# Two key tiles per P-times-V burst, and turns of four key tiles, in an attention and gated-FFN kernel

## The chip, the cores and the metric

The kernel runs on one core of one Trainium2 chip. The metric is the device time of one execution in microseconds (us). The engines are TensorE (PE, with its weight loads as PEld), VectorE (DVE), ScalarE (ACT), GpSimd (POOL), and SyncE (SP), whose queue issues the DMAs.

## The reference

One transformer block with adaptive layer norm, 2048 rows of 512, 32 heads of 16, one shared key and value head, and a gated FFN of width 1792 without a nonlinearity:

```python
mod = (silu(c) @ w_mod)                       # sa, ca, ga, sb, cb, gb
h = layernorm(x) * (1 + ca) + sa
q = (h @ wq) in 32 heads of 16;  k = h @ wk;  v = h @ wv      # k, v shared by the heads
p = softmax(q @ k.T / 4);  o = p @ v
x = x + ga * (o @ wo)
h = layernorm(x) * (1 + cb) + sb
x = x + gb * (((h @ w_gate) * (h @ w_up)) @ w_down)
```

## The kernel before, in words

**Units.** The attention is cut into NU = 32 units. A superblock is 256 queries (NS = 8 of them), and each has NC = 4 units of 8 heads. A unit passes over KT = 16 key tiles of 128 keys. For one key tile it needs four score products (two values of `p`, and two row groups `a` of the PE array: `a` = 0 is array rows 0 to 63, `a` = 1 rows 64 to 127), each 512 columns wide. ACT takes the exponential of each into one of eight SBUF buffers called `P` (`qk_exp`, L648 to L663). Then follow four products of V with those P tiles, which use all 128 rows and 32 columns each, so that the four run side by side (`pv`, L665 to L671). They are float32, and the profile counts two matmuls for each: a burst for one key tile is eight matmuls.

**Max.** Softmax needs the row maximum before the exponential. It comes from a second set of score products with queries as the output rows (`max_mm`, L593 to L611), whose 128 x 512 results DVE reduces (L605). They run about one unit ahead, and `flat` is the list of these steps. There are four of them for each key tile, as many as score products.

**Side products.** All other matrix products (the Q projection, the output projection `wo`, the FFN's gate and up `gu`, and its down product `down`) are cut into `Group`s (L491 to L538). A group accumulates into one PSUM bank, `n` steps on the upper and `n` on the lower row group of the array: 12 each for a `gu`, `wo` or Q group, 42 for a `down` group. One step on one row group is a "half". While row group 0 does score and max products, row group 1 does halves of a side group, and the two run at the same time. When a group goes on in the other row group than before, its first half there waits for an exponential of the turn before (`tc.add_manual_dep`, L527), so that the two row groups never write one bank at once. When a group has ended, `finish` gives it to its eviction: for a `gu` group ACT's copy L847, DVE's product L849, and POOL's L850 and L851.

**The order of the work.** It is written out by hand. `attend` (L1218) emits two key tiles in two turns. A string gives the order in a turn: `m` is a max product, `e` a score product with its exponential, `x` a side half; the digit is the row group, flipped in the second turn.

```python
MANY = "x1 e0 x1 m0 x1 e0 x1 e0 x1 m0 x1 m0 x1 m0 x1 e0"
```

So a turn in this style is eight slots, each with a half on one row group and an `m` or `e` on the other, and then `end_turn` emits the burst of one key tile. With `FEW` and `NO_SIDE`, used while the Q projections run or when no side group may begin, both row groups do `m` and `e`. `hooks` hangs the smaller work on fixed steps: weight preparation, and at `NORM_AT` the four parts of normalising the finished unit, whose P-times-V result `pv_out` has evicted. When `flat` is used up (in the last unit), `m` places take halves of a second group.

**PSUM.** All eight banks (NBANK) are in one queue, `pool` (L77 to L97). `ps_hold` takes the bank at the head and keeps it until `ps_give` appends it at the tail; `ps_mx` takes the head and appends it at once, so that score and max tiles rotate: a tile takes the bank of the tile as many places earlier as there are banks in the queue, and its matmul waits until the exponential or the reduce of that earlier tile is done. Held are one bank for the P-times-V result and one for each open side group, until its eviction has been emitted. `side_half` (L1203) keeps at most one group open in `cur`.

**Where the end comes from.** After the last unit a tail does the rest of the side products, with whole steps over all 128 rows.

Of the kernel before, what the change touches and what calls it, by code (L numbers as in the profile page):

```python
# [43 lines left out]
Q_LAG = 8  # L44
TR_WAIT = 11
NHF = 12
# [10 lines left out]

NO_SIDE = ("m0 m0 e1 m0 e1 e0 m1 e0 v", "e0 m1 m0 m1 e1 m1 e0 v e1")
FEW = "e1 m0 e0 x1 m0 x1 e0 x1 m0 x1 e1 m0"
MANY = "x1 e0 x1 m0 x1 e0 x1 e0 x1 m0 x1 m0 x1 m0 x1 e0"  # L60


@with_exitstack
def adaln_mqa_glu_kernel(ctx: ExitStack, tc: tile.TileContext, x_in, wq_in, wk_in, wv_in, wo_in,
# [35 lines left out]
        return ps_mx("misc", shape)  # L100


    c4 = consts.tile([KC, 128], F32, name="c4")
    nc.sync.dma_start(c4, c_in.rearrange("o (k p) -> (o k) p", p=128))
    wmA = big.tile([128, KC, 1536], F32, name="wmA", tag="wg")
# [7 lines left out]
    xbig = big.tile([128, 6, 2, D], F32, name="xbig", tag="wu")  # L113
    xts = [[xbig[:, i, t] for t in range(2)] for i in range(6)]
    for i in range(6, 8):
        xts.append([work.tile([128, D], F32, name="P", tag="P", bufs=8) for _ in range(2)])
# [12 lines left out]
    hf3 = [work.tile([128, BT], F32, name="P", tag="P", bufs=8) for k in range(KC)]  # L129
# [93 lines left out]
    h16 = big.tile([128, 2, KC, S], F16, name="h16", tag="big")  # L223
    kwb = big.tile([128, 2 * FT * D], F16, name="kwb", tag="wd")
    hfs = kwb[:, 0:2 * NHF * BT].bitcast(F32).rearrange("p (n t) -> p n t", n=NHF)
    ssqs = [kwb[:, 2 * n * BT:2 * n * BT + 2 * F].bitcast(F32) for n in (KC, 2 * KC)]
    kng = kwb[:, 2 * NHF * BT:2 * NHF * BT + BT]

# [412 lines left out]

    pvb = {}
    ptl = {}
    oc = {}
    och = {}
    pd = {}

    def qk_exp(u, kt, p, a, last=False):  # L648
        s = sst[u % 3]
        ptl[u, kt, p, a] = work.tile([128, D], F32, name="P", tag="P", bufs=8)  # L650
        t = ps_sc()
        keys = kst[64 * a:64 * a + 50, kt * 128:(kt + 1) * 128]
        if pending and last:
            for c in range(2):
                if c:
                    flush()
                nc.tensor.matmul(t[:, c * ST:(c + 1) * ST], keys, s[64 * a:64 * a + 50, c, p, :], start=True, stop=True)  # L657
        else:
            nc.tensor.matmul(t.rearrange("k (c n) -> k c n", c=2), keys, s[64 * a:64 * a + 50, :, p, :],  # L659
                             start=True, stop=True)  # L660
        ex = nc.scalar.activation(ptl[u, kt, p, a], t, AF.Exp)  # L661
        if sync["due"]:
            sync.update(due=False, exp=ex.ins.name)  # L663

    def pv(u, kt):  # L665
        if kt == 0:
            pvb[u] = ps_hold("pv")
        for j in range(4):
            p, a = divmod(j, 2)
            nc.tensor.matmul(pvb[u][32 * j:32 * j + 32, :], vst[:, kt, :], ptl[u, kt, p, a],  # L670
                             start=(kt == 0), stop=(kt == KT - 1))  # L671

    def pv_out(u):
        sb, ch = divmod(u, NC)
# [53 lines left out]
    def load_x(t):  # L728
        if t < KT - 2:
            x1s[t] = work.tile([128, D], F32, name="x1", tag="x1", bufs=6)  # L730
        else:
            x1s[t] = work.tile([128, D], F32, name="x1p", tag="P", bufs=8)
        nc.sync.dma_start(x1s[t], x_rows[t * 128:(t + 1) * 128, :])

    def wo_work(sb):
# [56 lines left out]
    def ln2_work(sb):  # L792
        st = {}

        def tr(i):
            def f():
                if not h2s:
                    h2T = big.tile([128, 2, 2, KC, ST], F16, name="h2T", tag="wq")
                    glus.append(big.tile([128, 2, 2, FT, ST], F16, name="glu", tag="big"))
                    h2s.update({s: h2T[:, s % 2] for s in range(NS)})  # L800
                st["p"] = ps_hold("mx")
                for k in range(2):
                    for t in range(2):
                        c = k * ST + t * 128
                        nc.tensor.transpose(st["p"][:, c:c + 128],  # L805
                                            n2s[2 * sb + t][:, (2 * i + k) * 128:(2 * i + k + 1) * 128], ident)
            return f

        def ev(i):
            def f():  # L810
                hf = work.tile([128, 2, ST], F32, name="hf", tag="g", bufs=2)
                for k in range(2):
                    nc.scalar.activation(hf[:, k, :], st["p"][:, k * ST:(k + 1) * ST], AF.Identity,  # L813
                                         bias=hsc[:, 2 * i + k, 0:1], scale=hsc[:, 2 * i + k, 1:2])
# [78 lines left out]
    def late_weights():  # L893
# [37 lines left out]
        def stage(n):  # L931
            if "d" in W:
                t = work.tile([128, D], F32, name="wsl", tag="xl", bufs=3)
            else:
                t = hfs[:, SLOTS[taken[0] % len(SLOTS)], :]
                taken[0] += 1
            nc.sync.dma_start(t[:, :sl[n][3]], sl[n][2])
            st[n] = t
# [262 lines left out]
    nrm = []  # L1201

    def side_half(r, cur=cur):  # L1203
        while True:
            if not cur:
                if cur is not second and second and second[0].turn != now[0]:
                    cur.append(second.pop())
                elif open_gate(now[0]):
                    cur.append(fill.popleft()[1])
                else:  # L1210
                    return
            if not cur[0].ended():
                break
            cur.clear()
        if cur[0].did[r] < cur[0].n:
            cur[0].half(r)

    def attend(u, kt):  # L1218


        now[0] = u * NSTEP + 2 * kt
        if cur and cur[0].ended():
            cur.clear()
# [5 lines left out]
        def end_turn(kt):  # L1229
            for g in ended:  # L1230
                g.finish()
            ended.clear()
            for f in ends:
                f()
            ends.clear()
            v = u * KT + kt - 1
            if v >= 0:
                pv(*divmod(v, KT))
                if v % KT == KT - 1:
                    ends.append(lambda: pv_out(u - 1))  # L1240
# [4 lines left out]
            hooks(u, 2 * kt + 1)  # L1245

        for turn in range(2):
            now[0] = u * NSTEP + 2 * (kt + turn)
            sync["before"] = sync["exp"]
            drain_posts()  # L1250
            order = orders[turn]
            for j, (what, a) in enumerate(order):
                if j == len(order) // 2:
                    drain_posts()
                    if style is not NO_SIDE:
                        late_max()
                    hooks(u, 2 * (kt + turn))
                a = a if style is NO_SIDE else a ^ turn
                if what == "m" and mstep[a] >= len(flat) and style is MANY:
                    mstep[a] += 1  # L1260
                    side_half(a, second)
                elif what == "m":
                    max_half(a)
                    drain_relus()
                elif what == "v":
                    end_turn(kt + turn)
                elif what == "x":
                    side_half(a)
                    continue
                else:  # L1270
                    k = count[a] = count.get(a, -1) + 1
                    qk_exp(u, kt + (k // 2 if style is MANY else turn), k % 2, a, j == len(order) - 1)
                flush()
            assert not sync["due"]
            if style is not NO_SIDE:
                end_turn(kt + turn)

    def hooks(u, i):
        step = u * NSTEP + i
# [1 line left out]
            b1, k = later_h.popleft()  # L1281
            h_halves(b1, (k,))
        side_step(step)
        if u > 0 and i in NORM_AT:
            if i == NORM_AT[0]:
                nrm[:] = normalise(u - 1)
            nrm[NORM_AT.index(i)]()
        if i == 20 and u > 0 and u % NC == 0:
            sb = u // NC - 1
            left = list(fill)  # L1290
            fill.clear()
# [7 lines left out]
    for u in range(NU):  # L1299
        if u == 1:  # L1300
            side.extend(dlist)
        for kt in range(0, KT, 2):
            attend(u, kt)

    def drain_all():
        for t in sorted(timers):
# [4 lines left out]

    u = NU - 1

    pv(u, KT - 1)
    pv_out(u)
    sync["before"] = sync["exp"]
    begun = cur + second
# [59 lines left out]
```

## Time and profile before

| | |
|---|---|
| median of 3 runs | 1665.57 us (1664.92 to 1665.84) |
| profiled execution: span from first to last instruction | 1663.8 us (the page gives no other time for it) |
| PE busy | 1643.3 us, 99% |
| DVE busy | 1402.3 us, 84% |
| ACT busy | 1234.8 us, 74% |
| POOL busy | 523.5 us, 31% |

A group of instructions is shown as line, engine, operation, output<-inputs, shapes, count, then busy time and mean length of one, then the idle time of its engine just before and what ended it. In rows in order of time the first number is the start in us from the start of the span, the second the length; `x4` means that four of a kind were merged into one row, which then reaches from the first one's start to the last one's end. PE matmuls overlap (their ends are modelled), so the distance between starts tells more than the length. The superblocks' regular stage lies between 320 and 1497 us; max products end at 1497 us and the units at 1552 us.

### The profile page before, as it was taken

What the parts mean: (1) busy time and instruction counts of PE and PEld (TensorE: products, weight loads), DVE (VectorE), ACT (ScalarE), POOL (GpSimd) and SP (SyncE); (2) the same over time, 40 slices, a digit from 0 to 9 for tenths busy, and PEclk for the clock granted to TensorE, in tenths of its full rate; (3) what the DMA queues carried; (4) which work ended last, traced back from release to release, by engine and by line L of the source; (5) the groups of instructions that cost most, each with busy time, mean ns of one, the idle gap of its engine ahead of it and who ended that gap; (6) DMA issues with size and microseconds to landing.
All of it is one profiled execution on the core that took longest, in us unless ns stands there. A gap on an engine that the chain in (4) does not pass through costs nothing.

```text
span 1663.8 us, 39821 instructions
## 1 busy us (share of the span) xinstructions
PE 1643.3 (99%) x15677; PEld 747.1 (45%) x15677; DVE 1402.3 (84%) x2434; ACT 1234.8 (74%) x2389; POOL 523.5 (31%) x833
## 2 busy tenths in 40 slices
PE   8899999999999999999999999999999999999999
PEld 4333333355533554335543355434545345454776
DVE  7999999998998999899998999999998999980211
ACT  5688888888777877777877787777878777877300
POOL 4857537864841111301112011300113001210322
PEclk9999999999999999999999999999999999999999
DMA  6313313342210001000000000000000000000100
GB/s 237 108 59 100 95 43 120 96 129 80 77 51 24 18 12 32 19 32 20 20 26 23 25 13 24 26 25 26 20 29 15 26 22 20 26 14 21 33 13 14
DMA packets 66024, 75.39 MB, mean 45 GB/s; under 512 B 17702, under 2 KB 46634, under 8 KB 65836
## 3 DMA queue, kind: packets, MB, share of 16 engines
q1 hardware_dynamic: 63724, 72.26, 13.7%
q8 instruction: 123, 2.02, 0.5%
q10 hardware_dynamic: 2112, 0.59, 0.1%
q14 instruction: 65, 0.53, 0.1%
HBM read 55.51 MB, written 17.04 MB: 44 GB/s over the span
## 4 chain that ended last, share of the span: by engine, by line
PE 93%; ACT 2%; DVE 2%; DMA 1%; issue 1%; POOL 0%; SPq 0%; ACTq 0%; DVEq 0%
PE side L511 41%; PE pv L670 30%; PE mx L601 8%; PE sc L659 8%; PE sc L657 3%; ACT P L661 2%; DVE mpart L605 1%; DMA xbig<-in_A_x_dram 1%; PE mx L805 1%; PE mxt L629 0%; ACT hf L813 0%; PE sc L601 0%; DVE bs L248 0%; DMA kwb<-in_B_w_down_dram 0%; DMA wkv<-in_A_wv_dram 0%
## 5 line engine op out<-in xcount | busy, mean ns | idle before, releaser
L605 DVE TENSOR_REDUCE mpart<-mx 128x1 f32<-128x512 f32 x2016 | 1274.1, 684 | 104.0 <-PE mx L601 95.7
L661 ACT ACTIVATE P<-sc 128x512 f32<-128x512 f32 x2048 | 1094.8, 598 | 274.2 <-PE sc L659 226.9
L601 PE MATMUL mx<-kst,sst 48*128 48x512 f16 x2032 | 631.5, 377 | 3.8 <-ACT P L661 1.7
L659 PE MATMUL sc<-sst,kst 50*128 50x512 f16 x1792 | 597.5, 379 | 0.6 <-ACT P L661 0.3
L670 PE MATMUL pv<-P,vst 128*32 128x512 f32 x4096 | 545.3, 605 | 0.7
L511 PE MATMUL side<-h2T,wg 64*128 64x256 f16 (+1 forms) x2396 | 540.8, 271 | 0.1
L511 PE MATMUL side<-h2T,wu 64*128 64x256 f16 (+1 forms) x2396 | 538.7, 270 | 0.0
L511 PEld LDWEIGHTS <-wg 64*128 64x128 f16 (+1 forms) x2396 | 226.0, 94 | 230.5 <-ACT P L661 194.0
L511 PE MATMUL side<-wd,glu 64*128 64x512 f16 (+1 forms) x1172 | 272.8, 378 | 0.2 <-ACT P L661 0.2
L850 POOL TENSOR_SCALAR glu<-gf 128x256 f16<-128x256 f32 x112 | 45.8, 409 | 671.3 <-DVE gf L849 583.9
L511 PEld LDWEIGHTS <-wu 64*128 64x128 f16 (+1 forms) x2396 | 226.4, 94 | 43.0 <-issue 7.8
L601 PEld LDWEIGHTS <-sst 48*128 48x128 f16 x2064 | 189.9, 94 | 34.2 <-issue 17.4
L659 PEld LDWEIGHTS <-kst 50*128 50x128 f16 x1792 | 162.9, 94 | 63.0 <-issue 50.3
L511 PEld LDWEIGHTS <-glu 64*128 64x128 f16 (+1 forms) x1172 | 98.5, 94 | 192.4 <-ACT P L661 85.9
L670 PEld LDWEIGHTS pv<-P,vst 128*32 128x32 f32 x4096 | 80.7, 108 | 160.9 <-issue 150.1
L849 DVE TENSOR_TENSOR gf<-side,g 128x256 f32<-128x256 f32 x112 | 46.7, 418 | 79.8 <-ACT g L847 77.7
L657 PE MATMUL sc<-sst,kst 50*128 50x256 f16 x512 | 96.9, 268 | 0.1
L511 PE MATMUL side<-h,wq 64*128 64x512 f16 (+1 forms) x372 | 95.0, 376 | 0.4 <-ACT P L661 0.4
L847 ACT ACTIVATE g<-side 128x256 f32<-128x256 f32 x112 | 42.3, 379 | 65.6 <-PE side L511 65.3
L511 PE MATMUL side<-wo,och 64*128 64x512 f16 (+1 forms) x360 | 86.3, 377 | 0.0
L851 POOL TENSOR_TENSOR glu<-gf,glu 128x256 f16<-128x256 f32 x112 | 75.3, 673 | 9.3
L706 POOL TENSOR_TENSOR oc<-oc,rr 128x256 f32<-128x256 f32 x31 | 22.7, 731 | 146.6 <-DMA rr<-ri 100.4
(233 smaller groups left out, 865.4 us busy)
## 6 DMA issues: line engine op xcount, KB each, us to landing
pd<-ev SPq DMA_DIRECT2D x32, 256.0 KB
kwb<-in_B_w_gate_dram SPq DMA_DIRECT2D x32, 224.0 KB
kwb<-in_B_w_up_dram SPq DMA_DIRECT2D x32, 224.0 KB
sst<-qd SPq DMA_DIRECT2D x180, 32.0 KB
qd<-q SPq DMA_DIRECT2D x16, 256.0 KB
oc<-pd SPq DMA_DIRECT2D x64, 64.0 KB
rr<-ri SPq DMA_DIRECT2D x64, 64.0 KB
x<-in_A_x_dram SPq DMA_DIRECT2D x14, 256.0 KB
```

What stands on the lines that cost most here:

```text
L511: return nc.tensor.matmul(self.p[:, c * w:(c + 1) * w], left[rows], right[rows], start=start and c == 0, stop=stop and c == len(terms) - 1)
L601: nc.tensor.matmul(m, s[64 * a:64 * a + 48, t // 2, p, t % 2 * 128:(t % 2 + 1) * 128], w[64 * a:64 * a + 48, :], start=(i == 0), stop=(i = ...
L605: nc.vector.tensor_reduce(part, m, axis=AX.X, op=OP.max)
L657: nc.tensor.matmul(t[:, c * ST:(c + 1) * ST], keys, s[64 * a:64 * a + 50, c, p, :], start=True, stop=True)
L659: nc.tensor.matmul(t.rearrange("k (c n) -> k c n", c=2), keys, s[64 * a:64 * a + 50, :, p, :], start=True, stop=True)
L661: ex = nc.scalar.activation(ptl[u, kt, p, a], t, AF.Exp)
L670: nc.tensor.matmul(pvb[u][32 * j:32 * j + 32, :], vst[:, kt, :], ptl[u, kt, p, a], start=(kt == 0), stop=(kt == KT - 1))
L706: eng.tensor_tensor(o, o, st["r"], op=OP.mult)
L847: nc.scalar.activation(g, p[:, 0:ST], AF.Copy, scale=2.0 ** -45)
L849: nc.vector.tensor_tensor(gf, p[:, ST:2 * ST], g, op=OP.mult)
L850: nc.gpsimd.tensor_scalar(glu()[:, 0, f, :], gf, 1.0, 0.0, op0=OP.mult, op1=OP.add)
L851: nc.gpsimd.tensor_tensor(glu()[:, 1, f, :], gf, glu()[:, 0, f, :], op=OP.subtract)
```

## The change

A third order for a turn is added, used in place of `MANY` at every fourth key tile once eight more P buffers exist. A turn then covers four key tiles of one row group in sixteen slots; the two turns of a pair emit two key tiles of P times V each, one right behind the other.

- `QUAD` alternates `m` and `e`, with a half before each. Half way through a turn `end_turn` is called as well, without P times V: it finishes ended groups and emits `pv_out`. The burst at the end of the first turn is that of the last two key tiles of the group of four before; that at the end of the second is of the first two of its own.
- The P buffers become sixteen: eight as before, by number (`p_tile`, `p_free`), and eight (`MORE_P`) in the space of `h16` (`tag="big"`), which the FFN's `glu` takes over when the Q projections are done. To make room `glu` becomes one buffer for all superblocks in place of two in turn.
- `side_half` keeps up to two groups open: when a row group has no steps left in the open ones, it begins the next group.
- In the first `QUAD` pair four more side halves and max products (`SKEW`) go in front of the second turn, so that one row group stays four steps ahead.
- `NORM_AT` counts from the step at which `pv_out` was emitted. Two staging slots for weights move (`SLOTS`).

```diff
-SLOTS = (0, 1, 2, 3, 6, 7)
+SLOTS = (0, 1, 2, 3, 12, 13)
-NORM_AT = (5, 12, 15, 19)
+NORM_AT = (2, 9, 12, 16)
+MORE_P = 8
+SKEW = 4
+QUAD = " ".join(["x1 m0 x1 e0"] * 8)
...
+    p_free = deque(range(8))
...
     def qk_exp(u, kt, p, a, last=False):
-        ptl[u, kt, p, a] = work.tile([128, D], F32, name="P", tag="P", bufs=8)
+        n = p_free.popleft()
+        ptl[u, kt, p, a] = (n, p_tile(n) if n < 8 else p_more[n - 8])
...
-                    glus.append(big.tile([128, 2, 2, FT, ST], F16, name="glu", tag="big"))
+                    both = big.tile([128, 2 * KC * S], F16, name="glu", tag="big")
+                    n = 2 * FT * ST
+                    glus.append(both[:, :n].rearrange("p (h f t) -> p h f t", h=2, f=FT))
+                    more = both[:, n:n + MORE_P * 2 * D].bitcast(F32).rearrange("p (n d) -> p n d", d=D)
+                    p_more.extend(more[:, i] for i in range(MORE_P))
+                    p_free.extend(range(8, 8 + MORE_P))
...
-            return glus[0][:, sb % 2]
+            return glus[0]
...
     def side_half(r, cur=cur):
-        while True:
-            if not cur:
-                if cur is not second and second and second[0].turn != now[0]:
-                    cur.append(second.pop())
-                elif open_gate(now[0]):
-                    cur.append(fill.popleft()[1])
-                else:
-                    return
-            if not cur[0].ended():
-                break
-            cur.clear()
-        if cur[0].did[r] < cur[0].n:
-            cur[0].half(r)
+        cur[:] = [g for g in cur if not g.ended()]
+        todo = [g for g in cur if g.did[r] < g.n]
+        if not todo and len(cur) < 2:
+            if cur is not second and second and second[0].turn != now[0]:
+                todo.append(second.pop(0))
+            elif open_gate(now[0]):
+                todo.append(fill.popleft()[1])
+            cur.extend(todo)
+        if todo:
+            todo[0].half(r)
...
+        if style is MANY and kt % 4 == 0 and p_more:
+            style = QUAD
+        length = 2 if style is QUAD else 1
...
+        if style is QUAD and mstep[1] < len(flat):
+            orders[1] = [("x", 1), ("m", 0)] * skew[0] + orders[1]
+            skew[0] = 0
...
-            v = u * KT + kt - 1
-            if v >= 0:
+            for v in range(next_pv[0], upto + 1):
                 pv(*divmod(v, KT))
...
+            parts = {len(order) * n // (2 * length): n for n in range(1, 2 * length)}
             for j, (what, a) in enumerate(order):
-                if j == len(order) // 2:
+                if j in parts:
                     drain_posts()
...
+                    else:
+                        end_turn(i + parts[j] - 1, next_pv[0] - 1)
...
             if style is not NO_SIDE:
-                end_turn(kt + turn)
+                end_turn(i + 2 * length - 1, u * KT + kt + (2 * turn if style is QUAD else turn) - 1)
...
-        if u > 0 and i in NORM_AT:
+        since = i - out_at[0]
+        if u > 0 and i >= 3 and since in NORM_AT:
```

More of the change, by code (lines that the diff above doesn't have):

```diff
@@ L100, in ps_misc, with p_tile @@
         return ps_mx("misc", shape)
+    def p_tile(n):
+        return work.tile([128, D], F32, name="P", tag=f"P{n}", bufs=1)
     c4 = consts.tile([KC, 128], F32, name="c4")
@@ L115, in adaln_mqa_glu_kernel @@
     for i in range(6, 8):
-        xts.append([work.tile([128, D], F32, name="P", tag="P", bufs=8) for _ in range(2)])
+        xts.append([p_tile(2 * (i - 6) + t) for t in range(2)])
     wqst = [work.tile([128, D], F32, name="wqst", tag="gf", bufs=4) for k in range(KC)]
@@ L128, in adaln_mqa_glu_kernel @@
         nc.sync.dma_start(wqst[k], wq_in[k * 128:(k + 1) * 128, :])
-    hf3 = [work.tile([128, BT], F32, name="P", tag="P", bufs=8) for k in range(KC)]
+    hf3 = [p_tile(4 + k) for k in range(KC)]
     wq = big.tile([128, 2, KC, D], F16, name="wq", tag="wq")
@@ L669, in pv @@
             p, a = divmod(j, 2)
-            nc.tensor.matmul(pvb[u][32 * j:32 * j + 32, :], vst[:, kt, :], ptl[u, kt, p, a],
-                             start=(kt == 0), stop=(kt == KT - 1))
+            n, t = ptl.pop((u, kt, p, a))
+            nc.tensor.matmul(pvb[u][32 * j:32 * j + 32, :], vst[:, kt, :], t, start=(kt == 0), stop=(kt == KT - 1))
+            p_free.append(n)
     def pv_out(u):
@@ L731, in load_x @@
         else:
-            x1s[t] = work.tile([128, D], F32, name="x1p", tag="P", bufs=8)
+            x1s[t] = p_tile(KT - 1 - t)
         nc.sync.dma_start(x1s[t], x_rows[t * 128:(t + 1) * 128, :])
@@ L934, in stage @@
             else:
[L935 removed]
+                t = stg[:, SLOTS[taken[0] % len(SLOTS)], :]
                 taken[0] += 1
@@ L1244, in end_turn @@
                 posts.append(post)
-            hooks(u, 2 * kt + 1)
+            hooks(u, i)
         for turn in range(2):
-            now[0] = u * NSTEP + 2 * (kt + turn)
+            i = 2 * (kt + length * turn)
+            now[0] = u * NSTEP + i
             sync["before"] = sync["exp"]
@@ L1271, in attend @@
                     k = count[a] = count.get(a, -1) + 1
-                    qk_exp(u, kt + (k // 2 if style is MANY else turn), k % 2, a, j == len(order) - 1)
+                    qk_exp(u, kt + (k // 2 if style in (MANY, QUAD) else turn), k % 2, a, j == len(order) - 1)
                 flush()
@@ L1301, in adaln_mqa_glu_kernel @@
             side.extend(dlist)
-        for kt in range(0, KT, 2):
-            attend(u, kt)
+        kt = 0
+        while kt < KT:
+            kt += attend(u, kt)
     def drain_all():
@@ L1312, in adaln_mqa_glu_kernel @@
     u = NU - 1
-    pv(u, KT - 1)
+    for v in range(next_pv[0], NU * KT):
+        pv(*divmod(v, KT))
     pv_out(u)
```

34 lines of the change are left out of this document (21 added, 13 removed).

## The prediction

> **What bounds the kernel now.** I read the page's busy times first, then the steady stage by windows, then single turns in order of time, each number below being in us.
>
> ```profile
> span 1663.8 us, 39821 instructions
> ...
> PE 1643.3 (99%) x15677; PEld 747.1 (45%) x15677; DVE 1402.3 (84%) x2434; ACT 1234.8 (74%) x2389; POOL 523.5 (31%) x833
> ...
> L605 DVE TENSOR_REDUCE mpart<-mx 128x1 f32<-128x512 f32 x2016 | 1274.1, 684 | 104.0 <-PE mx L601 95.7
> L661 ACT ACTIVATE P<-sc 128x512 f32<-128x512 f32 x2048 | 1094.8, 598 | 274.2 <-PE sc L659 226.9
> ```
>
> TensorE is never idle for long, and the max reduce alone makes 1274 of VectorE's 1402. The regular stage, 320 to 1497, and the last unit, which has no max products, by windows; then the same window for the instructions of tile `pv` alone:
>
> ```profile
> 320.00:1497.00 1177.00, 1173.83 (x11946) 538.59 (x11940) 1077.63 (x1817) 931.26 (x1801) 282.79 (x465) 1.00 0.11 32
> 1497.00:1552.00 55.00, 55.00 (x558) 24.70 (x555) 4.02 (x9) 42.44 (x81) 4.99 (x9) 1.00 0.05 16
> ```
> ```profile
> 320.00:1497.00 1177.00, 428.88 (x3224) 63.28 (x3216) 17.11 (x25) 1.00 0.11 32
> ```
>
> 3224 matmuls of eight to a burst are 403 bursts, so a turn takes 1177/403 = 2.92. DVE (the third busy time) works 1077.6 of 1177, 92%. PE sets the pace, and DVE is close behind. One ordinary turn of it:
>
> ```profile
> 901.77 0.39 PE L511 MATMUL side<-wd,glu 64*128 64x512 f16 x1
> 901.77 0.39 PE L659 MATMUL sc<-sst,kst 50*128 50x512 f16 x1
> ...
> 902.00 0.38 PE L601 MATMUL mx<-kst,sst 48*128 48x512 f16 x1
> ...
> 902.23 2.17 ACT L661 ACTIVATE P<-sc 128x512 f32<-128x512 f32 x4 [0.67 <-PE sc L659]
> ...
> 902.44 2.53 DVE L605 TENSOR_REDUCE mpart<-mx 128x1 f32<-128x512 f32 x4 [0.30 <-PE mx L601]
> ...
> 903.30 0.38 PE L659 MATMUL sc<-sst,kst 50*128 50x512 f16 x1
> ...
> 903.61 1.07 PE L670 MATMUL pv<-P,vst 128*32 128x512 f32 x8
> ...
> 904.61 0.39 PE L511 MATMUL side<-wd,glu 64*128 64x512 f16 x1
> ```
>
> From the first pair at 901.77 to that of the next turn it is 2.84. Eight slots start 0.217 apart (901.77 to 903.30 are seven steps), the burst starts 0.31 after the last slot, and the next pair 1.00 after the burst. A reduce starts 0.44 after its matmul (902.00 to 902.44), an exponential 0.46 after (901.77 to 902.23). Four reduces take 2.53, so they follow each other every (2.53 - 0.684)/3 = 0.62 (0.684 is the mean length of one), and exponentials every (2.17 - 0.598)/3 = 0.52. DVE idles 0.30 in the turn. It can go on through the burst because `MANY` puts three of its four max products into slots 4 to 6: three reduces are still to do when PE turns to P times V.
>
> **What the burst saves.** The very end of the attention has two key tiles behind one another already:
>
> ```profile
> 1549.70 0.27 PE L511 MATMUL side<-h2T,wu 64*128 64x256 f16 x1
> 1549.90 1.92 PE L670 MATMUL pv<-P,vst 128*32 128x512 f32 x16
> 1551.76 0.28 PE L511 MATMUL side<-h2T,wg 64*128 64x256 f16 x1
> ```
>
> Sixteen matmuls take 1.86 to the next side matmul. Two single bursts cost 2 x (0.31 - 0.217 + 1.00) = 2.19 beyond their slots, a double one 0.31 - 0.217 + 1.86 = 1.95: 0.24 less. A `QUAD` turn without any stall is 15 x 0.217 + 0.31 + 1.86 = 5.43, against 2 x 2.84 = 5.68. If that were all, some 201 pairs of turns in the stage and 9 in the last unit would give 210 x 0.25 = 53.
>
> **What the banks allow.** The new order puts max products into all even slots (0 to 14) and score products into all odd ones, and each takes the next bank of the queue. Eight banks less one for P times V are six with one open side group and five with two. The trace shows what a queue of five does. These are rows of a turn in which a group ended and the next was begun, so that two were held, and below it the turn before, with one held:
>
> ```profile
> 1008.48 0.38 PE L601 MATMUL mx<-kst,sst 48*128 48x512 f16 x1
> ...
> 1008.74 2.20 ACT L661 ACTIVATE P<-sc 128x512 f32<-128x512 f32 x4 [0.71 <-PE sc L659]
> ...
> 1008.90 0.69 DVE L605 TENSOR_REDUCE mpart<-mx 128x1 f32<-128x512 f32 x1 [0.31 <-PE mx L601]
> ...
> 1009.36 0.27 PE L511 MATMUL side<-h2T,wg 64*128 64x256 f16 x1
> 1009.39 0.37 PE L601 MATMUL mx<-kst,sst 48*128 48x512 f16 x1
> ...
> 1009.57 0.27 PE L511 MATMUL side<-h2T,wg 64*128 64x256 f16 x1
> 1009.64 0.37 PE L601 MATMUL mx<-kst,sst 48*128 48x512 f16 x1
> ```
> ```profile
> 1006.05 1.94 DVE L605 TENSOR_REDUCE mpart<-mx 128x1 f32<-128x512 f32 x3 [0.31 <-PE mx L601]
> ...
> 1006.73 0.37 PE L601 MATMUL mx<-kst,sst 48*128 48x512 f16 x1
> 1006.73 0.27 PE L511 MATMUL side<-h2T,wg 64*128 64x256 f16 x1
> ```
>
> The max product of slot 6 went out at 1009.64, 0.07 after its side partner at 1009.57 and 0.05 after the end of the reduce that began at 1008.90 (1009.59): five places earlier is the tile of slot 1. That of slot 5 waited for slot 0's exponential (1008.74 + 0.60 = 1009.34, out at 1009.39). In the turn before, slot 6 and its partner go out together at 1006.73, before slot 1's reduce has ended at 1006.74. So the rotation binds, with 0.05 from release to matmul; under `MANY` it costs hundredths.
>
> Under `QUAD` max products come every 0.43 and DVE takes 0.62. A reduce starts 0.42 (1008.48 to 1008.90) to 0.44 after its matmul. With the turn's first slot at 0, reduce j ends at D(j) = 0.43 + 0.685 + 0.62 j = 1.115 + 0.62 j.
> - Queue of six: a max tile takes the bank of the max tile three before. The last (j = 7) waits for D(4) + 0.05 = 3.645, where its slot was 3.04. The score product follows at 3.86, and the next turn begins at 3.86 + 0.31 + 1.86 = 6.03.
> - Queue of five: a score tile takes the bank of the max tile m(j-2). The last waits for D(5) + 0.05 = 4.265, and the next turn begins at 6.44.
>
> Nor does this even out over the turns: after the last slot only two or three reduces are left, at most 1.6 of work, while the burst and the way to the next reduce take 0.31 + 1.86 + 0.43 = 2.60. DVE, with nothing to read, idles about 1.0 in each turn; what was a burst of PE becomes a hole in DVE. The stalled matmul stands at the head of PE's queue, with the halves of the other row group behind it.
>
> **How often five.** With `SKEW` a `gu` group of 12 steps ends four times in six turns. The second bank is then held from slot 12 of the first turn, through the first half of the second, from slot 8 of the third through half of the fourth, from slot 4 to 8 of the fifth, and from slot 12 of the sixth. In the first, third and sixth turn the last slots have five: 6.44. In the second, fourth and fifth `finish` falls into the middle, where the bank comes back but the group's DVE product stands between the fourth and the fifth reduce:
>
> ```profile
> L849 DVE TENSOR_TENSOR gf<-side,g 128x256 f32<-128x256 f32 x84 | 34.9, 416 | 0.7 <-ACT g L847 0.2
> ...
> L847 ACT ACTIVATE g<-side 128x256 f32<-128x256 f32 x84 | 31.7, 378 | 0.0
> ...
> L511 PE MATMUL side<-h2T,wg 64*128 64x256 f16 x2016 | 456.8, 270 | 0.1
> ...
> L511 PE MATMUL side<-wd,glu 64*128 64x512 f16 x864 | 207.5, 377 | 0.2 <-ACT P L661 0.2
> ...
> L511 PE MATMUL side<-wo,och 64*128 64x512 f16 x288 | 69.4, 377 | 0.0
> ```
>
> The product waits for ACT's copy, and that stands behind the fourth exponential, which ends at 0.217 + 0.46 + 3 x 0.52 + 0.60 = 2.84: copy until 3.2, product until 3.6, and D(4), 0.62 behind it, becomes 4.2 in place of 3.6. So the last max product goes out at 4.25, and the turn takes 4.25 + 0.217 + 2.17 = 6.63. A mean of 6.54 for `gu`, and for `wo`, whose groups are as long. A `down` group of 42 steps has the queue of six nearly always, 6.03. By the halves in these rows, 2016 `gu` (one `wg` and one `wu` matmul each), 864 `down` and 288 `wo` of 3168, the mean is 0.73 x 6.54 + 0.27 x 6.03 = 6.40.
>
> What is in the stage beside turns (the transposes of the FFN's input and of the maxima, and waits for them) I take from the chain of waits in 904 to 1091:
>
> ```profile
> by line: PE side L511 39.6%; PE pv L670 34.6%; PE mx L601 10.7%; PE sc L659 8.0%; PE sc L657 4.0%; ACT P L661 1.4%; ACT hf L813 0.7%; PE mx L805 0.6%; PE mxt L629 0.4%; issue 0.2%
> ```
>
> L805, L629 and L813 are 1.7%, 20 of 1177. Stage after: 201.5 x 6.40 + 20 = 1310, or +133. The last unit keeps the plain gain, 9 x 0.25 = 2. So 1663.8 + 131 = 1795 for the span; the median of the runs stood 1.8 above that span, within the rounding here.
>
> **The rest of the change, and what hides it.** Twice as many P buffers are filled before each burst frees eight; the first exponential of a turn needs one of them, and its score product stands behind the burst on PE anyway: 0. The first half of a turn waits for the last exponential of the turn before, which ends 0.46 + 0.60 after slot 15, covered by 0.31 + 1.86: 0, and the 1.4% of ACT waits in the last row (16) may go; I count that in the range only. The single `glu` buffer makes POOL's first write of a superblock wait for the last reads of `down`, which stand in front of it in side order; POOL is 31% busy: 0, and without that cover some 10 per superblock at the wait for a group's bank. `NORM_AT` and `SLOTS` move DMAs by a few steps on the SP queue, a unit ahead of their use: 0. Halves lost where `down` may not begin until all `gu` have ended: up to 12 of 0.217 a superblock, done in the tail instead at half price, 6 x 1.3 = 8 at most.
>
> **The rivals.**
> 1. *Six banks nearly always.* If the second group is open seldom or its bank comes back in time: 201.5 x 6.03 + 20 = 1235, +58 - 2: 1720. For it: `down` turns. Against: the count of steps above.
> 2. *Faster: the banks do not bind.* One mechanism: when the burst begins, four reduces are still unread, so DVE works through its 2.60 and PE never waits for a bank. That decides from eight banks in rotation on, where the last max product waits for D(3) + 0.05 = 3.03. Price -0.25 a pair: 1613. DVE's sum would allow it, since 1077.6 is below 1177 - 50. Against it stands the matmul at 1009.64.
> 3. *Seven banks' worth of slack* (P times V's bank or the early halves help): the last score product waits for D(4) + 0.05, the turn is 5.82, and 201.5 x 5.82 + 20 = 1193: +16 - 2, 1678. Around it lies no change.
> 4. *The clock falls.* Two windows of the start, where PE waited for the layer norm:
>
> ```profile
> 54.00:56.00 2.00, 0.37 (x2) 0.13 (x3) 2.00 (x4) 0.00 (x0) 1.92 (x3) 0.82 0.00 0
> 56.00:58.00 2.00, 2.00 (x12) 0.94 (x10) 2.00 (x5) 1.47 (x3) 1.92 (x3) 0.50 0.00 0
> ```
>
> After 1.6 of 2 idle the granted clock was 0.50. The new stalls are 0.2 to 0.4 each, with matmuls between, so I expect the 1.00 of the stage's row above throughout. If instead each of 25 units lost 6 at half clock, 25 x 3 = 75 more: 1870. The Trainium skill, "TensorE: Matmul & The Clock Gate", section "A second HAM failure mode: psum-queue depth-cycling", says that a kernel cycling through PSUM banks idled in short pieces between matmul groups, often enough for its clock to swing; by that rule this rival is the likely one. No row of the kernel before has such stalls for long, so only the changed kernel can show it.
>
> **How the numbers follow.** The forecast (queue of five under `gu`) has 0.60, from 1745 to 1840; rival 1 0.18; rival 2 0.12; rival 3 0.05; the clock 0.03; no change 0.02. Likeliest time 1795. The range 1675 to 1840 holds the forecast and rivals 1 and 3. A difference of 0.2% (3.3) is about what a measurement of this kernel can tell from none: faster 0.12, same 0.03, slower 0.85.
>
> **What would show it.** In the changed profile: bursts of sixteen with 1.86 to the next pair (the saving is real); `QUAD` turns of 6.0 to 6.6 with max and score matmuls leaving late by 0.2 from slot 8 on, 0.05 after a reduce has ended; DVE idle about 1 a turn, in front of L605, released by PE; DVE's share below 84%. Turns of 5.4 to 5.5 with DVE busy through the burst would make me wrong, and so would score tiles that wait for ACT in place of DVE.

## The result, and the profile after

| | before | after |
|---|---|---|
| median | 1665.7 us (1664.92 to 1666.19, 4 runs) | 1796.19 us (1794.49 to 1797.75, 4 runs) |
| ratio | | 1.0784, 95% interval 1.0768 to 1.0799 |
| span of the profiled execution | 1663.8 us | 1792.7 us |
| from 320 us to the last max product | 1177.6 us | 1303.6 us |
| from the last max product to the end | 166.2 us | 169.1 us |

The changed kernel is 130 us slower, and 126 us of it lie in the regular stage. These are the page's busy times after, and the row of the max reduce:

```profile
span 1792.7 us, 39273 instructions
...
PE 1735.5 (97%) x15566; PEld 764.4 (43%) x15566; DVE 1376.7 (77%) x2434; ACT 1223.2 (68%) x2389; POOL 523.6 (29%) x833
...
PE 71%; DVE 20%; ACT 5%; issue 2%; DMA 1%; POOL 0%; SPq 0%; ACTq 0%; DVEq 0%
```

PE looks busy at 97% still, because ends of matmuls are modelled and overlap; the chain of waits (last row) is more telling: DVE's share of it was 2% and is 20%. The stage by windows (first the length, then the busy time of PE, PEld, DVE, ACT and POOL, then the granted clock), and the group of max reduces in it:

```profile
320.00:1623.00 1303.00, 1263.30 (x11786) 551.56 (x11782) 1051.92 (x1817) 920.15 (x1796) 282.10 (x464) 1.00 0.09 29
```
```profile
L612 DVE TENSOR_REDUCE mpart<-mx 128x1 f32<-128x512 f32 x1607 | 992.3, 681 | 223.1 <-PE mx L608 223.0
```

and the same group of the kernel before, by lines of its window from 320 to 1497:

```profile
L605 DVE TENSOR_REDUCE mpart<-mx 128x1 f32<-128x512 f32 x1607 | 1019.4, 685 | 95.0 <-PE mx L601 88.6 <-PE side L511 2.5
```

The same 1607 reduces had 95 us of idle DVE in front of them and now have 223, nearly all waiting for a max matmul. These 128 us more are nearly the 126 that the stage grew by. The full account by the windows is this: DVE's idle time grew by 152 us (from 99 to 251), of which 128 stand before max reduces and 21 before the product of a `gu` group (L865), which waits for ACT's copy; its busy time fell by 26 (from 1077.63 to 1051.92), because reduces in a row overlap (they start 0.60 apart and last 0.68) and an overlap counts once. DVE's work did not grow; it got holes.

One ordinary turn of a `down` group shows the hole, first on PE. Max products (L608) and score products (L669) alternate, each beside a half (L518):

```profile
981.77 0.39 PE L518 MATMUL side<-wd,glu 64*128 64x512 f16 x1
981.77 0.39 PE L608 MATMUL mx<-kst,sst 48*128 48x512 f16 x1
...
983.57 0.37 PE L608 MATMUL mx<-kst,sst 48*128 48x512 f16 x1
...
984.17 0.37 PE L608 MATMUL mx<-kst,sst 48*128 48x512 f16 x1
984.17 0.39 PE L518 MATMUL side<-wd,glu 64*128 64x512 f16 x1
...
984.77 0.37 PE L608 MATMUL mx<-kst,sst 48*128 48x512 f16 x1
984.77 0.39 PE L518 MATMUL side<-wd,glu 64*128 64x512 f16 x1
...
985.36 0.37 PE L608 MATMUL mx<-kst,sst 48*128 48x512 f16 x1
985.37 0.39 PE L518 MATMUL side<-wd,glu 64*128 64x512 f16 x1
...
985.58 0.38 PE L669 MATMUL sc<-sst,kst 50*128 50x512 f16 x1
985.88 1.06 PE L681 MATMUL pv<-P,vst 128*32 128x512 f32 x8
986.77 1.04 PE L681 MATMUL pv<-glu,vst 128*32 128x512 f32 x8
987.74 0.39 PE L518 MATMUL side<-wd,glu 64*128 64x512 f16 x1
```

and then the reduces of this turn and the next on DVE:

```profile
982.23 3.68 DVE L612 TENSOR_REDUCE mpart<-mx 128x1 f32<-128x512 f32 x6 [1.10 <-PE mx L608]
985.82 0.24 DVE L704 RECIPROCAL rc<-rc 128x16 f32<-128x16 f32 x1
985.98 1.22 DVE L612 TENSOR_REDUCE mpart<-mx 128x1 f32<-128x512 f32 x2
988.20 4.88 DVE L612 TENSOR_REDUCE mpart<-mx 128x1 f32<-128x512 f32 x8 [0.99 <-PE mx L608]
```

From the fifth on the max matmuls leave 0.60 apart, which is DVE's pace ((4.88 - 0.68)/7), where the order would have them 0.43 apart; a half that stands behind one in PE's queue leaves with it. When the burst starts at 985.88, DVE has two reduces and a small one left, is done at 987.20, and then has nothing until 988.20. The turn takes 5.97 us, the double burst 1.86 of it (985.88 to 987.74), as the end of the old kernel had shown.

The mean lengths of the double turns in the stage, from the starts of the first pairs (turns with only one kind of side product and without a transpose in them), beside the forecast:

| side product | forecast us | measured us | turns |
|---|---|---|---|
| `gu` | 6.54 | 6.46 | 92 |
| `down` | 6.03 | 6.07 (5.97 is the commonest) | 33 |
| `wo` | 6.54 | 6.39 | 12 |

These are 137 of the stage's 200 double turns. The 26 others with two kinds of side product take 6.67 in the mean, and the 37 with a transpose 6.93.

### The profile page after: what moved, and what is told of

The parts are those of the page before. It is cut to its first block, busy times and chain, and to the rows that moved or that the text cites. A ratio compares the mean times of both kernels' runs of the same rounds, so it can differ in the third digit from the quotient of the medians.

```text
span 1792.7 us, 39273 instructions
## 1 busy us (share of the span) xinstructions
PE 1735.5 (97%) x15566; PEld 764.4 (43%) x15566; DVE 1376.7 (77%) x2434; ACT 1223.2 (68%) x2389; POOL 523.6 (29%) x833
## 4 chain that ended last, share of the span: by engine, by line
PE 71%; DVE 20%; ACT 5%; issue 2%; DMA 1%; POOL 0%; SPq 0%; ACTq 0%; DVEq 0%
PE pv L681 26%; PE side L518 24%; DVE mpart L612 17%; PE sc L669 9%; PE mx L608 8%; ACT P L671 2%; PE sc L667 2%; ACT glu L671 2%; DVE gf L865 1%; ACT g L863 1%; DMA xbig<-in_A_x_dram 1%; PE mx L821 0%; DVE x L761 0%; DVE bs L768 0%; PE sc L608 0%
## 5 line engine op out<-in xcount | busy, mean ns | idle before, releaser
L612 DVE TENSOR_REDUCE mpart<-mx 128x1 f32<-128x512 f32 x2016 | 1246.8, 681 | 232.7 <-PE mx L608 230.7
L671 ACT ACTIVATE P<-sc 128x512 f32<-128x512 f32 x1200 | 658.4, 604 | 348.0 <-PE sc L669 300.3
L608 PE MATMUL mx<-kst,sst 48*128 48x512 f16 x2032 | 748.4, 378 | 17.5 <-DVE mpart L612 15.4
L669 PE MATMUL sc<-sst,kst 50*128 50x512 f16 x1919 | 706.9, 376 | 20.7 <-DVE mpart L612 7.0
L518 PE MATMUL side<-h2T,wu 64*128 64x256 f16 (+1 forms) x2402 | 566.5, 272 | 0.0
L518 PE MATMUL side<-h2T,wg 64*128 64x256 f16 (+1 forms) x2402 | 559.1, 270 | 1.4 <-POOL h2T L835 0.6
L671 ACT ACTIVATE glu<-sc 128x512 f32<-128x512 f32 x848 | 486.4, 607 | 79.4 <-PE sc L669 50.4
L681 PE MATMUL pv<-P,vst 128*32 128x512 f32 x2400 | 404.0, 601 | 0.2
L518 PEld LDWEIGHTS <-wu 64*128 64x128 f16 (+1 forms) x2402 | 226.0, 94 | 198.3 <-issue 163.0
L681 PE MATMUL pv<-glu,vst 128*32 128x512 f32 x1696 | 309.0, 597 | 0.0
L518 PE MATMUL side<-wd,glu 64*128 64x512 f16 (+1 forms) x1176 | 287.0, 379 | 0.0
L518 PEld LDWEIGHTS <-wg 64*128 64x128 f16 (+1 forms) x2402 | 227.3, 95 | 127.7 <-issue 72.9
L608 PEld LDWEIGHTS <-sst 48*128 48x128 f16 x2064 | 189.9, 94 | 52.5 <-issue 34.3
L669 PEld LDWEIGHTS <-kst 50*128 50x128 f16 x1919 | 174.8, 94 | 74.5 <-issue 53.8
L518 PEld LDWEIGHTS <-glu 64*128 64x128 f16 (+1 forms) x1176 | 94.4, 94 | 175.7 <-issue 99.8
L865 DVE TENSOR_TENSOR gf<-side,g 128x256 f32<-128x256 f32 x112 | 47.4, 424 | 101.3 <-ACT g L863 80.2
L518 PE MATMUL side<-h,wq 64*128 64x512 f16 (+1 forms) x372 | 95.0, 376 | 0.4 <-ACT P L671 0.4
L518 PE MATMUL side<-wo,och 64*128 64x512 f16 (+1 forms) x360 | 93.8, 379 | 0.0
L681 PEld LDWEIGHTS pv<-glu,vst 128*32 128x32 f32 x1696 | 65.9, 109 | 56.1 <-issue 56.1
```

Of the source, the lines that this page charges most:

```text
L518: return nc.tensor.matmul(self.p[:, c * w:(c + 1) * w], left[rows], right[rows], start=start and c == 0, stop=stop and c == len(terms) - 1)
L608: nc.tensor.matmul(m, s[64 * a:64 * a + 48, t // 2, p, t % 2 * 128:(t % 2 + 1) * 128], w[64 * a:64 * a + 48, :], start=(i == 0), stop=(i = ...
L612: nc.vector.tensor_reduce(part, m, axis=AX.X, op=OP.max)
L671: ex = nc.scalar.activation(ptl[u, kt, p, a][1], t, AF.Exp)
L865: nc.vector.tensor_tensor(gf, p[:, ST:2 * ST], g, op=OP.mult)
```

## The experiments

The theory under test: the long burst leaves DVE without max tiles, because five or six banks in rotation cannot hold enough of them, and PE then waits for banks at DVE's pace. The rivals: the other parts of the change (two open groups, one `glu` buffer, sixteen P buffers) cost the time; or long turns and bursts do so by themselves, on PE.

### The new order never used

```diff
-        if style is MANY and kt % 4 == 0 and p_more:
+        if style is MANY and kt % 4 == 0 and p_more and False:
```

> The change with its third order never used, so single bursts and eight-slot turns throughout; two open groups, the single glu buffer, the sixteen P buffers and the moved parts of normalising stay. Bank theory (the new order leaves DVE without tiles during the long burst): the loss goes, 1655 to 1680 us. A turn of the old order keeps 2.84 us, 2.94 where two groups are open by my recurrence for five banks. Rival (the other parts of the change cost the time, above all two open groups and the single glu buffer): 1740 to 1800 us.

Measured: 1663.17 us, ratio to before 0.9987, interval 0.9978 to 0.9996. All of the loss belongs to the new order. The rest of the change even gains 0.13%. The tail has 270 whole `gu` steps in place of 292, at about 0.22 us each, so fewer slots stayed empty in the stage; that this is the whole of the gain was not tried.

### The new order where there are no max products

```diff
-        if style is MANY and kt % 4 == 0 and p_more:
+        if style is MANY and kt % 4 == 0 and p_more and min(mstep) >= len(flat):
```

> The new order used only when the max products are used up, which is in the last unit. There the changed kernel took 38.1 us for the unit and the kernel before 41.5 us. Bank theory: DVE has nothing to do there, so long bursts pay: 3 us below the same kernel without the new order, about 1660 us, faster than before by 0.1 to 0.3%. Rival (long bursts or sixteen-slot turns cost by themselves): no gain or a loss against the run without the new order.

Measured: 1662.45 us, ratio 0.9981, interval 0.9972 to 0.9989. That is 0.2% below the kernel before. But against the kernel without the new order it is 0.7 us, with overlapping runs (1661.22 to 1663.57 against 1662.71 to 1663.84), where I expected 3. By the time alone this is nearer to the rival's "no gain". The turns say more: an undisturbed double turn takes 5.45 us there, against 2 x 2.84, so long bursts do no harm where DVE has nothing to do; but of the last unit's turns only some are of that length, and from the end of the turn with the last max product to the last P times V it takes 51.4 us in place of 52.3. The 38.1 against 41.5 us that the expectation went by compared units from one eviction of P times V to the next, and under the new order that eviction comes later in the unit: here the last unit shrank from 41.2 to 37.9 us and the one before it grew from 45.8 to 48.1.

### Another order of the sixteen slots

```diff
-QUAD = " ".join(["x1 m0 x1 e0"] * 8)
+QUAD = "x1 m0 x1 e0 x1 m0 x1 e0 x1 e0 x1 m0 x1 e0 x1 m0 x1 e0 x1 m0 x1 e0 x1 m0 x1 e0 x1 m0 x1 m0 x1 e0"
```

> The changed kernel with another order of the same sixteen slots: m e m e e m e m e m e m e m m e, so one max product more stands among the last four slots and is still to be read when the burst begins. Nothing else differs. Bank theory, by the same recurrence as in the prediction: a turn of 6.10 us with five banks in rotation in place of 6.43, and 5.81 with six in place of 6.03; over 201 turns some 55 us less than the changed kernel, 1725 to 1755 us, and still slower than before. Rival (the length of the turn, the second open group or the P buffers cost the time): within 10 us of 1796.

Measured: 1744.36 us, ratio 1.0474, interval 1.0458 to 1.0490; 52 us less than the changed kernel by the order of slots alone. An ordinary `down` turn takes 5.75 us (forecast 5.81), `gu` turns 6.17 in the mean. On DVE, two turns of it:

```profile
964.24 4.88 DVE L612 TENSOR_REDUCE mpart<-mx 128x1 f32<-128x512 f32 x8 [0.78 <-PE mx L608]
969.99 0.69 DVE L612 TENSOR_REDUCE mpart<-mx 128x1 f32<-128x512 f32 x1 [0.88 <-PE mx L608]
```

The eight reduces end at 969.12, and the next starts at 969.99. The hole has gone from 1.10 to 0.88 (from 0.99 to 0.78 where the small reciprocal falls into it), and the turn has become 0.22 shorter. Sixteen slots and a double burst are the same as in the changed kernel, so they are not what cost these 52 us.

### A shorter reduce, in both kernels

```diff
-            nc.vector.tensor_reduce(part, m, axis=AX.X, op=OP.max)
+            nc.vector.tensor_reduce(part, m[:, 0:256], axis=AX.X, op=OP.max)
...
-        ex = nc.scalar.activation(ptl[u, kt, p, a][1], t, AF.Exp)
+        ex = nc.scalar.activation(ptl[u, kt, p, a][1], t, AF.Exp, scale=1.0 / 64.0)
```

> The changed kernel with the max taken over 256 of 512 keys of each tile, so a DVE reduce of about 0.42 us (DVE's product over 256 columns took 0.42) in place of 0.68, one every 0.35. What is left out: half of the keys in the max, and the exponent is scaled by 1/64 so that nothing overflows. Matmuls and ACT's work are the same. Bank theory: banks come back soon, ACT's 0.52 us for an exponential binds instead, a turn of 5.6 to 5.8 us in place of 6.0 to 6.6: 1640 to 1670 us. Rival (the loss is PE's own: row switches, weights, length of turns; or the second open group by itself): above 1750 us.

> The kernel before with the same half reduce (half of the keys left out of the max, the exponent scaled by 1/64). Bank theory: PE sets the pace there already, a turn stays at 2.84 us, and only the few hundredths where a group changes go: 1645 to 1664 us, within 15 us of the changed kernel with the half reduce. If DVE had been the bound of the kernel before, it would fall by 50 us or more.

Measured, one execution each: 1679.29 us for the changed kernel, 117 less than with the whole reduce, and 1652.21 us for the kernel before, 14 less. So DVE's time decides about the changed kernel and hardly about the old one. The first is 9 us above the upper end of what I expected, and the gap between the two is 27 us where I had said 15. The rows of DVE and PE between 400 and 1500 in the changed kernel with the short reduce show why:

```profile
L612 DVE TENSOR_REDUCE mpart<-mx 128x1 f32<-128x256 f32 x1483 | 602.7, 421 | 360.4 <-PE mx L608 336.3 <-PE side L518 6.7
L865 DVE TENSOR_TENSOR gf<-side,g 128x256 f32<-128x256 f32 x74 | 31.4, 425 | 67.6 <-ACT g L863 67.6
```
```profile
L669 PE MATMUL sc<-sst,kst 50*128 50x512 f16 x1373 | 516.3, 376 | 20.0 <-DVE gf L865 17.9 <-ACT ev L687 1.6 <-ACT glu L671 0.4
```

The reduce takes 0.42 us as estimated, and DVE idles a great deal. But the product of a group that was finished in the middle of a turn (L865) waits 0.9 us for ACT's copy, which stands behind the exponentials, and score products now wait for the bank that this product gives back. I had left that wait out. `down` turns, which have no such eviction, take 5.57 us in the mean and 5.50 mostly (expected from 5.6 on), `gu` turns 5.99 (expected up to 5.8). Of 92 `gu` turns the 40 with a product between the fourth and the fifth reduce take 6.33 in the mean, the other 52 take 5.74: 0.59 in each of the 40, or 24 us in these turns alone, of a gap of 27. That this closes the gap was not tried: no run has both the short reduce and evictions at the end of a turn only.

### One bank less, in both kernels

From the first FFN transpose on, at about 313 us:

```diff
                 if not h2s:
+                    pool.popleft()
```

> The changed kernel with one PSUM bank taken out of the rotation for good when the first FFN input is transposed (about 313 us), where the new order begins. Bank theory: five and four banks in place of six and five. By the recurrence 6.43 in place of 6.03 us a turn for down groups, and 6.65 and more (6.75 with the product in the middle) in place of 6.54 for gu: 30 to 60 us more, 1825 to 1860 us. Rival (DVE's sum of work or PE's own time binds, not the number of banks): within 5 us of 1796.

> The kernel before with the same bank taken out from the same place on. Bank theory: five banks in place of six, and four where a group changes. By the recurrence an old turn goes from 2.84 to 2.94 us, and up to 3.46 in part of every third: 40 to 70 us more, 1705 to 1735 us. Rival (the kernel before has banks to spare): within 5 us of 1666.

Measured, one execution each: 1871.11 us for the changed kernel, 75 more, and 1746.0 us for the old one, 80 more. Both are 11 us above the upper end of what I expected. The ordinary `down` turns are where the recurrence had them: 6.35 us in the changed kernel (forecast 6.43), 2.95 in the old one (forecast 2.94). What I had too low are the `gu` turns. In the old kernel I had put "part of every third" at up to 3.46; 73 of the 219 `gu` turns, a full third, take over 3.2 us, 3.40 in the mean (4 of 219 did before), and `gu` turns make 42 of the 80 us. In the changed kernel they went from 6.46 to 6.81 where I had 6.65 to 6.75. The twelve turns of the old kernel with a transpose of the FFN's input, which holds one more bank, went from 3.77 to 4.04, which is 3 us in all. A turn of the old order with five banks on PE, and its reduces:

```profile
921.96 0.37 PE L659 MATMUL sc<-sst,kst 50*128 50x512 f16 x1
...
922.59 0.38 PE L511 MATMUL side<-wd,glu 64*128 64x512 f16 x1
922.71 0.37 PE L601 MATMUL mx<-kst,sst 48*128 48x512 f16 x1
```
```profile
921.96 2.53 DVE L605 TENSOR_REDUCE mpart<-mx 128x1 f32<-128x512 f32 x4 [0.42 <-PE mx L601]
```

The first of the four reduces ends at 921.96 + 0.68 = 922.64, and the matmul of slot 6 leaves at 922.71, 0.12 after its partner. That is the wait which the prediction had found in group changes, now in an ordinary turn. So the old kernel had no bank to spare either; its order just fits six.

### One open group

```diff
-        if not todo and len(cur) < 2:
+        if not todo and len(cur) < 1:
```

> The changed kernel with one side group open at a time in place of two. Six banks stay in rotation, but a row group that has finished its steps of the open group leaves its slots empty: by counting slots some 350 halves of gu groups go to the tail, 0.108 us each, +38 us. Bank theory: turns with gu products come down from 6.46 us in the mean to 6.0 to 6.25, 30 to 55 us less in the stage; together 1760 to 1800 us. Rival (the second group's bank does not matter): gu turns stay at 6.4 to 6.5 and the time rises to 1825 to 1840 us.

Measured, one execution: 1792.73 us. `gu` turns go from 6.46 to 6.29 us in the mean, so the second group's bank is worth 0.17 a turn, less than expected, and the tail takes it back: 344 whole `gu` steps in place of 286 and 252 `down` steps in place of 168. Holding two groups was about even here. The mean stays above 6.03 because groups are still evicted in the middle of a turn: the 34 `gu` turns with a product between the fourth and the fifth reduce take 6.59 in the mean, the 38 without any product 5.96. The next run takes that product out of the middle, with two groups open as in the changed kernel.

### Eviction at the end of a turn only

```diff
-        def end_turn(i, upto):
-            for g in ended:
+        def end_turn(i, upto, finish=True):
+            for g in ended if finish else ():
                 g.finish()
-            ended.clear()
+            if finish:
+                ended.clear()
...
-                        end_turn(i + parts[j] - 1, next_pv[0] - 1)
+                        end_turn(i + parts[j] - 1, next_pv[0] - 1, False)
```

> The changed kernel with ended groups evicted at the end of a turn only, not in its middle. By the recurrence the DVE product no longer stands between the fourth and the fifth reduce, and a gu turn where a group ends takes 6.44 us in place of 6.63, against a bank held for half a turn longer: 10 to 20 us less, 1776 to 1786 us. Rival (the product in the middle costs nothing, the banks alone decide): 1796 us or some us more, since a bank is held longer.

Measured, one execution: 1771.83 us, 24 less than the changed kernel (I had said 10 to 20). `gu` turns take 6.29 us in the mean in place of 6.46. These are DVE's rows of a `gu` turn of the changed kernel with the eviction in its middle:

```profile
1013.57 2.48 DVE L612 TENSOR_REDUCE mpart<-mx 128x1 f32<-128x512 f32 x4 [1.07 <-PE mx L608]
1016.29 0.42 DVE L865 TENSOR_TENSOR gf<-side,g 128x256 f32<-128x256 f32 x1 [0.23 <-ACT g L863]
1016.63 2.47 DVE L612 TENSOR_REDUCE mpart<-mx 128x1 f32<-128x512 f32 x4
1020.17 4.88 DVE L612 TENSOR_REDUCE mpart<-mx 128x1 f32<-128x512 f32 x8 [1.07 <-PE mx L608]
```

Four reduces, 0.23 of waiting for ACT's copy, the product, and only then the other four; and the hole of 1.07 behind them all the same. At the end of the turn the product lies in that hole, as the run's own rows show for a turn of 6.32 us:

```profile
1002.65 4.87 DVE L612 TENSOR_REDUCE mpart<-mx 128x1 f32<-128x512 f32 x8 [0.79 <-PE mx L608]
1007.76 0.42 DVE L865 TENSOR_TENSOR gf<-side,g 128x256 f32<-128x256 f32 x1 [0.24 <-ACT g L863]
1008.97 4.87 DVE L612 TENSOR_REDUCE mpart<-mx 128x1 f32<-128x512 f32 x8 [0.79 <-PE mx L608]
```

### The new order in the last unit, and another order of the old turn

The kernel with the new order in the last unit only, and with another order of the old turn:

```diff
-MANY = "x1 e0 x1 m0 x1 e0 x1 e0 x1 m0 x1 m0 x1 m0 x1 e0"
+MANY = "x1 e0 x1 m0 x1 e0 x1 m0 x1 e0 x1 m0 x1 m0 x1 e0"
```

> The kernel with the new order in the last unit only, and in all other units another order of the old turn's eight slots: e m e m e m m e for e m e e m m m e. Bank theory: with six or five banks the recurrence gives the same turn (2.83 and 2.94 us), with four 3.31 for 3.46; four are in rotation only for a few slots where a group changes while the maxima are transposed. 0 to 4 us below 1662.5, still faster than before. Rival (the order of slots matters by more than the banks): a change of over 5 us either way.

Measured: 1661.43 us, ratio 0.9975, interval 0.9965 to 0.9984. It is 4 us, a quarter of a per cent, below the kernel before, the least of all versions here that compute the whole block. Against the same kernel with the old turn's order (1662.45) the 1.0 us is within the spread of the runs.

## Why the prediction came out

It was right in direction, in cause and in size: 1795 forecast, 1796.19 measured.

**The burst.** The double burst takes the 1.86 us read from the end of the old attention, and the saving exists: where the max products are used up a double turn takes 5.45 us, forecast 5.43. In the stage the hole on DVE outweighs it.

**The banks.** The recurrence gave 6.03 and 6.44 us from a slot of 0.217, a reduce each 0.62 and 0.05 from release to matmul. Ordinary `down` turns take 5.97: backlogged reduces follow each other every 0.60. The 2.53 of four reduces in the old turn, from which I took 0.62, held a small wait for PE: the second reduce starts 0.65 after the first, 0.44 after its matmul, and the others 0.60 apart. With 0.60 the recurrence gives 5.95 and 6.33; the commonest `down` turn takes 5.97, the commonest `gu` turn 6.32. The hole on DVE, forecast at about 1.0, is 0.99 to 1.10. The runs with another order, with a shorter reduce and with a bank less each moved the turns to where the same recurrence puts them, within 0.1 us for turns without an eviction. For the cause this is more than the argument of the prediction: less DVE time and better placed max products each help, a bank less hurts, and the long turn with the double burst does no harm where there are no max products. What stays open is the share of each of the two things that `QUAD` changes at once, the longer pause and the places of the max products. Another order of the slots alone gave 52 of the 130 us back; no run has single bursts with the alternating order.

**The share of five banks.** This was the weakest step and came out a little too high: 6.54 forecast for `gu`, 6.46 measured. The product in the middle of a turn was priced at 0.19 in half of the turns. Taking it away changed the mean by 0.17 and the kernel by 24 us, more than the 0.095 that half of 0.19 makes. What was too small is the difference and not the turn with the product: the 40 of 92 `gu` turns that have it between the fourth and the fifth reduce take 6.67 in the mean (forecast 6.63), but the other 52 take 6.30 and not 6.44, by the pace of 0.60. The price is 0.37 in 40 of 92 turns, or 0.16 in the mean.

**The sum.** The stage was forecast at +133 us and came to +126. The last unit and the tail were forecast at -2 and came to +2.9. A part of both misses is where the boundary falls: counted to the end of the turn that holds the last max product (1499.55 us before, 1629.22 after), the stage grew by 129.7 and the rest became 0.8 shorter. Some luck is left. The turns of the table are shorter in sum than forecast, and turns with two kinds of side product, which had no term of their own, are longer; over all 200 double turns the mean is 6.50, and the forecast with its 20 us for transposes makes 1310/201.5 = 6.50. Also, 1795 was worked out as a span; the span came to 1792.7, and the median lies 3.5 above it. The distance of 1 us between forecast and median is better than its terms.

**What was costed at nothing.** Without the new order, the sixteen P buffers, the single `glu` buffer, the moved parts of normalising, the moved staging slots and the two open groups are together 2.7 us on the right side (1663.17 against 1665.90). Within the long turns only the second group was tried by itself. The wait of the product in the middle for ACT's copy had been counted in the turn of 6.63; the wait of a score product for the bank that it frees had no term, and it shows where the reduces are short.

**The rivals.** Six banks nearly always (1720) falls on the `gu` turns of 6.46. Banks that do not bind (1613) would have shown turns of 5.4, and seven banks' worth of slack (1678) turns of 5.82; the commonest `down` turn takes 5.97. The granted clock stayed at 1.00 in the stage (row of the windows above), with PE's next matmul held back by 0.2 to 0.4 us several times a turn. The Trainium skill, "TensorE: Matmul & The Clock Gate", section "A second HAM failure mode: psum-queue depth-cycling", tells of a kernel whose clock swung because TensorE idled in short pieces between groups of matmuls. This trace does not show that, but it is a weak test of it: matmuls overlap, and by the same row PE is busy for 1263.30 of the 1303 us.

## What to carry to other kernels

Merging short bursts on one engine saves its switching cost (here 0.23 us for two key tiles, 5.45 against 5.68), and makes the pause longer for every engine that lives on what it produces between bursts; before it is done, count the work that the buffers in between can hold when the burst begins (here two or three reduces of 0.6 us) against the pause (2.6 us with the way to the next reduce). With buffers that rotate through a queue, write down which tile takes whose place: from a handful of rows that gives the length of a turn to a few per cent, and one place in the trace where the wait already shows is enough to check it. Here the engine that was busy for 92% of the stage was the next bound, and the change of order cost the idle time that it put into this engine, not more work.

## What the runs showed of the hardware

The clock did not fall, as told above. Nothing else was unexpected beyond sizes: a 128x512 reduce from PSUM takes 0.68 us alone and 0.60 in a row, a 128x256 one 0.42, and a matmul leaves about 0.05 us after the reduce that frees its bank.
